# Units first in their step, a later combining pass, and a rearranged prologue in a fused spectral-mixing and ELU kernel

## The chip, the cores and the metric

The kernel runs on one core of a Trainium2 chip. The core has five engines with queues of their own: TensorE (PE in the profile, with its weight loads as PEld), VectorE (DVE), ScalarE (ACT), GpSimd (POOL) and SyncE (SP), the last of which only issues DMA transfers here. POOL and ACT issue some transfers too. Each engine works its own instructions in the order in which the program lists them; engines wait for each other by semaphores. The metric is device time in microseconds for one execution of the whole program.

## The reference

Two stages follow each other. The first takes x (8 batches, 3008 positions, 256 channels), transforms it along the positions, multiplies by a complex 256x256 matrix, adds a bias, shrinks each part towards zero by 0.01, and transforms back. The second is a two-layer network with an ELU between the layers, on all 24064 rows.

```python
X = np.fft.rfft(x, axis=1)                      # x: 8, 3008, 256
Yr = Xr @ w_r - Xi @ w_i + b_r
Yi = Xr @ w_i + Xi @ w_r + b_i
Yr = np.sign(Yr) * np.maximum(np.abs(Yr) - 0.01, 0.0)
Yi = np.sign(Yi) * np.maximum(np.abs(Yi) - 0.01, 0.0)
y = np.fft.irfft(Yr + 1j * Yi, n=3008, axis=1)
...
h = y.reshape(24064, 256) @ w_in                # w_in: 256, 2048
g = np.where(h > 0.0, h, np.exp(np.minimum(h, 0.0)) - 1.0)
out = g @ w_out                                 # w_out: 2048, 256
```

## The kernel before, in words

3008 is 47 x 64, and the transform is done in two short matrix products per direction. One batch goes through five kinds of units, each of which fills one PSUM slot of two banks with matmuls and has it emptied ("evicted") by another engine:

- A (`unit_A`, L112; 8 a batch): x times the table M1, two matmuls of 512 columns. ACT evicts to a tile A, and SP writes A to a DRAM buffer DA (L134, L136), two units a write.
- X (`unit_X`, L148; 6 a batch): a tile Z is read back from DA in another order (`load_Z`, L138), in three groups of eight frequencies; Z times the table M2, eight matmuls of 128 columns. ACT evicts to XT.
- M (`unit_M`, L183; 12 a batch, M(q, i)): XT times the complex weights wcat, four matmuls of 512 columns; DVE adds the bias (yb, L179), POOL clips and subtracts (L187, L188). Two M units share one PSUM slot.
- B (`unit_B`, L210; 6 a batch): the shrunk values times the table M3, eight matmuls on halves of the array's rows (64 rows each). ACT evicts to Bz, SP writes Bz to a DRAM buffer DB.
- Y (`unit_Y`, L252; 8 a batch): Bs is read back from DB (`load_Bs`, L243), Bs times M4, eight matmuls of 94 columns. ACT evicts to yT, which the second stage reads.

The second stage runs in 48 steps a batch (`PER`): six blocks of 512 rows (the last has 448), eight pairs of 128 hidden channels each. In step i, `front(i)` (L529) makes the hidden values hps of one pair with four matmuls of 512 columns, and ACT takes their exponential into Et (L547). `elu(i)` (L550) makes gT from both in two passes over 1024 elements on DVE: a first pass on Et alone (L558; in steps without a unit, L555 splits it between DVE and POOL) and a combining pass that reads hps too (L559 or L556) and so frees its PSUM slot. `back(i-2)` (L567) multiplies the gT of two steps ago by w_out into an accumulator ps_o (eight matmuls of 256 columns, L584). Every eighth step ACT copies ps_o to osb, and SP writes that out in four or five transfers.

hps has two PSUM slots, ps_o two of one bank each, and all the units together have one slot (`psF`). So a unit can start only when the one before it has been evicted, and hps of step i only when the combining pass of step i-2 is done.

The units of the next batch, and the A units of the one after that, are laid into the steps of this batch by `plan(b)` (L616), which gives each step three lists: f0 is issued ahead of `front`, f1 between `front` and `elu`, f2 behind `back` (the loop at L675 to L694). X and Y stand in f0; A, M and B in f1; the loads of Bs, the last loads of Z and one Y unit in f2. The order on each engine is the order in which this loop issues. In batch 0, two Y units, the eight A units of batch 1, four Y units and then the list `mid` follow each other, from step 1 on; the loads of x for batch 2 are listed in steps 13, 16, 19 and 22 (`xs`). POOL, which issues them, has nothing else to do before and reaches them early.

Ahead of the loop lies a prologue. POOL issues the loads of x for batch 0 and makes index tables; DVE makes phases from them (three groups, L383 to L395, with `wrap` for the range reduction), ACT the sines (L362); in between, the eight A units of batch 0 run. Then Z is loaded, and X, M and B of batch 0 run with eviction shared out between ACT and DVE (`fX`, `first_M`, `fB`, L466 to L500). Matmuls on dummy data (`idle_pe`) fill PE's waits. After B, Bs is loaded, the first two Y units run (L508), a gate on POOL (L511) waits for part of Bs, and behind it the four x tiles of batch 1 are loaded (L512).

Of the kernel before, what the change touches and what calls it, by code (L numbers as in the profile page):

```python
# [8 lines left out]
ALU = mybir.AluOpType  # L9
# [16 lines left out]
def kernel(  # L26
# [38 lines left out]
    xp = ctx.enter_context(tc.tile_pool(name="xp", bufs=4))  # L65
    wk2 = ctx.enter_context(tc.tile_pool(name="wk2", bufs=2))
# [27 lines left out]
    def load_x(b, ci):  # L94
        xv = x[b].rearrange("(r m c) d -> c r m d", c=4, m=8)
# [16 lines left out]
    def unit_A(b, u, alone=False, on_dve=False):  # L112
# [9 lines left out]
        dav = DA_of[b].rearrange("(m c) r d -> c r m d", c=4)  # L122
# [15 lines left out]
    def load_Z(b, g, engs=None):  # L138
        engs = engs or (nc.sync, nc.sync)
        Z = wk3.tile([P, 8, D], BF16, name="Z", tag="Z")  # L140
        for c in range(2):
            for h in range(2):
                r = h * 2 * K1 + c * K1 + 8 * g
                q = c * N2 + h * NH
                engs[c].dma_start(Z[q : q + NH], DA_of[b][:, r : r + 8, :])
        Z_of[b, g] = Z

    def unit_X(b, u, alone=False, on_dve=False):  # L148
# [3 lines left out]
        XT, Z = XT_of[b, g], Z_of[b, g]  # L152
        ps = unit_ps("xps", alone)
        psv = ps[:].rearrange("p a (k j) -> p (a k) j", j=P)
        for kk in range(8):
            nc.tensor.matmul(  # L156
                psv[:, kk, :], lhsT=Z[:, kk, dt * P : dt * P + P], rhs=M2[:, :, 8 * g + kk, :],
                start=True, stop=True,
            )
        evac(  # L160
            XT[:, dt].rearrange("p c (k j) -> p c k j", j=N2),
            psv.rearrange("p k (c j) -> p c k j", c=2), on_dve,
        )
# [79 lines left out]
    def load_Bs(b, w, engs=None):  # L243
        engs = engs or (nc.sync, nc.sync)
        Bs = wk4.tile([4 * K1, 8, D], BF16, name="Bs", tag="Bs")
        dv = DB_of[b].rearrange("k (c m) d -> (k c) m d", c=2)
        for h in range(2):
            n0 = h * NH + 8 * w
            engs[h].dma_start(Bs[h * 2 * K1 : h * 2 * K1 + 2 * K1], dv[:, n0 : n0 + 8, :])
        Bs_of[b, w] = Bs  # L250
# [28 lines left out]
    with tc.tile_pool(name="stagep", bufs=1) as stagep:  # L279
# [3 lines left out]
        w_r_f = stagep.tile([P, 2, D], F32, name="w_r_f")  # L283
        nc.sync.dma_start(w_r_f[:], w_r.rearrange("(c p) e -> p c e", p=P))
        w_i_f = stagep.tile([P, 2, D], F32, name="w_i_f")
        nc.sync.dma_start(w_i_f[:], w_i.rearrange("(c p) e -> p c e", p=P))
# [16 lines left out]

        pcol = iota([P, 1], "pcol", [[0, 1]], cm=1)
        k1row = iota([2 * N1, 2, K1], "k1row", [[0, 2], [1, K1]])
        ph1 = iota([2 * N1, 2, K1], "ph1", [[QUARTER, 2], [0, K1]], base=QUARTER)
        for ci in range(2):
            load_x(0, ci)
        kv = iota([P, K1, N2], "kv", [[1, K1], [N1, N2]])
        for ci in range(2, 4):  # L310
            load_x(0, ci)
# [413 lines left out]
```

## Time and profile before

| | us |
|---|---|
| median of three runs | 972.80 (972.73 to 973.07) |
| the profiled execution | 972.56 |
| its span in the profile | 970.8 |
| first hps matmul of the loop | 65.28 |
| first hps of batches 1, 2, 3, 4, 5, 6, 7 | 193.88, 307.40, 420.84, 534.30, 647.80, 761.27, 871.37 |
| busy time PE, DVE, ACT, POOL | 932.9, 799.6, 634.0, 316.7 |

A step is the time from one first hps matmul to the next. By these starts a steady batch takes 113.5 us, batch 0 128.6, batch 6 (which has no A units to run) 110.1, and batch 7 (which has only Y units) 99.4 with the end of the program. In a step, a busy time is not a limit in itself: the chain of waits tells which engine the next one waited for. Groups of PE matmuls overlap at their ends in the timeline, so slots on PE are read from the chain, or from start to start.

### The profile page before, as it was taken

Reading aid. Unit: us, or ns where it says so; the run is one execution under the profiler, and the core shown is the slowest. Engines: PE = TensorE matmul, PEld = TensorE weight load, DVE = VectorE, ACT = ScalarE, POOL = GpSimd, SP = SyncE. Lnnn points to the kernel's source line nnn. Section 1 sums busy time; section 2 is a strip of 40 time slices with the busy share of each in tenths; the row PEclk is TensorE's granted clock in tenths of the full one; section 3 lists DMA queues with packets and bytes.
Section 4 is the critical chain, followed back from the end, with each engine's and each line's share of the span. In section 5 each row is a group of like instructions: output and inputs, shape, how many; then the busy total and the mean of one; then the engine's idle time right before and its main releaser. Section 6 shows DMA issues by size and latency. Waiting matters only on the chain.

```text
span 970.8 us, 16851 instructions
## 1 busy us (share of the span) xinstructions
PE 932.9 (96%) x6507; PEld 659.5 (68%) x6507; DVE 799.6 (82%) x935; ACT 634.0 (65%) x724; POOL 316.7 (33%) x359
## 2 busy tenths in 40 slices
PE   6887999999999999999999999999999999999997
PEld 2445766676667766776667766777667776677775
DVE  8555888788878888888888888788888888888896
ACT  4445755876687666775676756876667756667564
POOL 4341155026402443117312264024431053321332
PEclk8898999999999999999999999999999999999999
DMA  9979461847157452755437482574517301331011
GB/s 192 266 158 206 120 109 48 200 113 130 54 147 162 77 88 59 191 106 86 83 97 200 70 132 55 139 167 76 93 52 194 78 22 51 89 80 42 23 44 41
DMA packets 115331, 105.43 MB, mean 109 GB/s; under 512 B 8242, under 2 KB 108084, under 8 KB 115252
## 3 DMA queue, kind: packets, MB, share of 16 engines
q1 hardware_dynamic: 87028, 76.05, 29.9%
q0 software_dynamic: 27680, 26.74, 20.5%
q10 hardware_dynamic: 544, 1.57, 0.6%
q8 instruction: 51, 0.84, 0.4%
q14 instruction: 28, 0.23, 0.1%
HBM read 54.53 MB, written 49.81 MB: 107 GB/s over the span
## 4 chain that ended last, share of the span: by engine, by line
PE 63%; DVE 19%; ACT 9%; issue 4%; DMA 3%; POOL 2%; DVEq 0%; ACTq 0%; POOLq 0%
PE ps_o L584 25%; PE hps L542 24%; DVE gT L556 7%; PE mps L172 7%; ACT Et L547 5%; DVE gT L559 3%; DVE Et L555 3%; PE xps L156 2%; DVE Et L558 2%; PE aps L125 2%; PE bps L220 2%; PE yps L260 1%; DVE yb L179 1%; DMA DA<-A 1%; ACT A L110 1%
## 5 line engine op out<-in xcount | busy, mean ns | idle before, releaser
L547 ACT ACTIVATE Et<-hps 128x1024 f32<-128x1024 f32 (+1 forms) x384 | 388.1, 1011 | 220.7 <-PE hps L542 217.1
L584 PE MATMUL ps_o<-w_out_r,gT 128*128 128x256 f32 (+1 forms) x3072 | 479.9, 299 | 1.1 <-DVE gT L556 1.0
L584 PEld LDWEIGHTS ps_o<-w_out_r,gT 128*128 128x128 f32 (+1 forms) x3072 | 408.9, 187 | 62.3 <-DVE gT L556 13.0
L542 PE MATMUL hps<-yT,w_in_s 128*128 128x512 bf16 (+1 forms) x1536 | 391.0, 377 | 3.6 <-DVE gT L556 1.0
L559 DVE SCALAR_TENSOR_TENSOR gT<-hps,Et 128x1024 fp32r<-128x1024 f32 (+1 forms) x287 | 348.9, 1216 | 24.4 <-DVE Et L558 0.5
L558 DVE TENSOR_SCALAR Et<-Et 128x1024 f32<-128x1024 f32 (+1 forms) x287 | 204.4, 712 | 86.3 <-ACT Et L547 82.4
L542 PEld LDWEIGHTS <-w_in_s 128*128 128x128 bf16 x1536 | 125.3, 98 | 108.6 <-issue 6.3
L187 POOL TENSOR_SCALAR clip<-yb 128x512 f32<-128x512 f32 x84 | 82.1, 977 | 324.1 <-DVE yb L179 322.2
L555 POOL TENSOR_SCALAR Et<-Et 128x512 f32<-128x512 f32 (+1 forms) x97 | 62.1, 640 | 262.0 <-ACT Et L547 262.0
L556 DVE SCALAR_TENSOR_TENSOR gT<-Et,hps 128x1024 fp32r<-128x1024 f32 (+1 forms) x97 | 112.6, 1160 | 21.2 <-POOL Et L555 11.0
L188 POOL TENSOR_TENSOR Y<-yb,clip 128x512 bf16<-128x512 f32 x84 | 108.5, 1292 | 7.0
L110 ACT CAST XT<-xps 128x1024 bf16<-128x1024 f32 x46 | 46.6, 1012 | 52.8 <-PE xps L156 52.8
L179 DVE TENSOR_TENSOR yb<-mps,bias_bc 128x512 f32<-128x512 f32 x96 | 65.6, 687 | 9.4 <-PE mps L172 5.1
L110 ACT CAST A<-aps 96x1024 bf16<-96x1024 f32 x63 | 62.9, 1003 | 13.0 <-PE aps L125 7.8
L172 PEld LDWEIGHTS <-XT 128*128 128x128 bf16 x384 | 37.3, 98 | 44.8 <-issue 1.4
L110 ACT CAST yT<-yps 128x752 bf16<-128x752 f32 x63 | 49.6, 788 | 25.5 <-PE yps L260 25.5
L125 PE MATMUL aps<-xt,M 94*96 94x512 f32 x128 | 50.2, 478 | 13.9 <-ACT A L110 10.1
L172 PE MATMUL mps<-wcat_r,XT 128*128 128x512 bf16 x192 | 57.6, 382 | 0.0
L172 PE MATMUL mps<-wcat_s,XT 128*128 128x512 bf16 x192 | 57.2, 380 | 0.0
L555 DVE TENSOR_SCALAR Et<-Et 128x512 f32<-128x512 f32 (+1 forms) x97 | 52.1, 537 | 2.7 <-ACT Et L547 2.7
L596 ACT COPY osb<-ps_o 128x512 f32<-128x512 f32 x88 | 47.5, 590 | 8.0 <-PE ps_o L584 8.0
L98 POOL DMA_DIRECT2D xt<-in_x_dram x64 | 44.3, 694 | 12.0 <-PE aps L125 11.6
(83 smaller groups left out, 338.9 us busy)
## 6 DMA issues: line engine op xcount, KB each, us to landing
xt<-in_x_dram POOLq DMA_DIRECT2D x32, 640.0 KB, 6.0
out_dram<-osb SPq DMA_DIRECT2D x160, 128.0 KB
Z<-DA SPq DMA_DIRECT2D x90, 128.0 KB
Bs<-DB SPq DMA_DIRECT2D x60, 192.0 KB
DA<-A SPq DMA_DIRECT2D x28, 384.0 KB
DB<-Bz SPq DMA_DIRECT2D x21, 512.0 KB
xt<-in_x_dram POOLq DMA_DIRECT2D x32, 112.0 KB, 5.7
w_in_f<-in_moe_w_in_dram SPq DMA_DIRECT2D x4, 512.0 KB
```

Source lines behind the costliest of these rows:

```text
L110: nc.scalar.copy(dst, src)
L172: nc.tensor.matmul(ps, lhsT=XT[:, dt, c, o : o + P], rhs=wm[:, dt, :], start=(m == 0 and dt == 0), stop=(m == 1 and dt == 1),)
L179: nc.vector.tensor_tensor(yb[:], ps, bias_bc[:], ALU.add)
L187: nc.gpsimd.tensor_scalar(clip[:], yb[:], LAM, -LAM, ALU.min, ALU.max)
L188: nc.gpsimd.tensor_tensor(Y_of[b, q][:, i, :], yb[:], clip[:], ALU.subtract)
L542: nc.tensor.matmul(hps[:, s, 0:nb], lhsT=w_in_s[:, dt, ft * P : ft * P + P], rhs=yT[:, dt, bs : bs + nb], start=(dt == 0), stop=(dt == 1),)
L547: nc.scalar.activation(Et[:, :, 0:nb], hps[:, :, 0:nb], AF.Exp)
L555: eng.tensor_scalar(E_[:, s], E_[:, s], 1.0, 0.0, ALU.min, ALU.max)
L556: nc.vector.scalar_tensor_tensor(gT[:, :, 0:nb], E_, -1.0, h_, ALU.add, ALU.max)
L558: nc.vector.tensor_scalar(E_, E_, 1.0, -1.0, ALU.min, ALU.add)
L559: nc.vector.scalar_tensor_tensor(gT[:, :, 0:nb], h_, 0.0, E_, ALU.max, ALU.add)
L584: nc.tensor.matmul(po[q][0 : t1 - t0, i_ % 2, :], lhsT=gT[:, s, t0:t1], rhs=w_out_r[:, ft, :], start=(ft == 0 and i_ % 2 == 0), stop=(ft = ...
```

## The change

1. Order in the loop. All units now stand in f0, ahead of `front`. The combining pass of step i-1 (`finish_elu`) is issued in step i, behind the units and `front`, so behind a bias pass of an M unit of step i; behind it comes the first pass of step i. f2 is gone: load_Bs follows A(2) and load_Z follows A(7), in f1.
2. Batch 0. The Y units 6 and 7 move from before X(0) of batch 1 to places between later units. A gate on POOL, which waits for the last group of Z of batch 1, stands ahead of the x loads of batch 2. Both of Y(1, 0) and Y(1, 1) are in f0.
3. Layout. The 32 rows that belong to one r are split into four consecutive runs of eight (`r c m`) instead of every fourth row (`r m c`). A tile of x then reads 8 KB in one piece per partition, and the rows of DA that one tile fills lie together (`c m`).
4. Prologue tables. The second phase table is made as an absolute value and a product with half the range (two operations of one pass) instead of a shift and a second `wrap`; all three groups come first on DVE, ahead of the small tables. The sines are issued in single halves between the A units. Of the x loads, only the first is ahead of the table kv on POOL.
5. Z is one tile of 24 frequencies for the whole batch (pool zp). In batch 0, its first half (from the first two tiles of A) is loaded on POOL's queue after A(3), the second in three groups on SP and ACT. The loads of w_r and w_i come after A(3), and their casts to wcat go from POOL to DVE.
6. In the prologue, each X eviction is split in halves between ACT and DVE, and X and M units alternate from M(0, 0) on. The first 16 frequencies of Bs for w = 0 and 1 are loaded before B(5), the rest after it.

```diff
     def load_x(b, ci):
-        xv = x[b].rearrange("(r m c) d -> c r m d", c=4, m=8)
+        xv = x[b].rearrange("(r c m) d -> c r m d", c=4, m=8)
...
-        dav = DA_of[b].rearrange("(m c) r d -> c r m d", c=4)
+        dav = DA_of[b].rearrange("(c m) r d -> c r m d", c=4)
...
-    def load_Z(b, g, engs=None):
-        engs = engs or (nc.sync, nc.sync)
-        Z = wk3.tile([P, 8, D], BF16, name="Z", tag="Z")
+    def load_Z(b, k0, k1, n0, n1, engs):
+
+        if b not in Z_of:
+            Z_of[b] = zp.tile([P, K1, D], BF16, name="Z", tag="Z")
         for c in range(2):
             for h in range(2):
-                r = h * 2 * K1 + c * K1 + 8 * g
+                r = h * 2 * K1 + c * K1
                 q = c * N2 + h * NH
-                engs[c].dma_start(Z[q : q + NH], DA_of[b][:, r : r + 8, :])
-        Z_of[b, g] = Z
+                engs[c].dma_start(
+                    Z_of[b][q + n0 : q + n1, k0:k1, :], DA_of[b][n0:n1, r + k0 : r + k1, :]
+                )
...
+        if alone:
+            nc.scalar.copy(xv[:, :, 0:4], pv[:, :, 0:4])
+            nc.vector.tensor_copy(xv[:, :, 4:8], pv[:, :, 4:8])
+        else:
+            nc.scalar.copy(xv, pv)
...
-    def load_Bs(b, w, engs=None):
+    def load_Bs(b, w, k0=0, k1=K1, engs=None):
...
-        for ci in range(2):
-            load_x(0, ci)
+        load_x(0, 0)
         kv = iota([P, K1, N2], "kv", [[1, K1], [N1, N2]])
-        for ci in range(2, 4):
+        for ci in range(1, 4):
             load_x(0, ci)
...
+        def phases(g):
+
+            gs = slice(8 * g, 8 * g + 8)
+            nc.vector.tensor_scalar(
+                v2[:, gs, :], kv[:, gs, :], n2col[:], ph2col[:], ALU.mult, ALU.add
+            )
+            nc.vector.tensor_scalar(
+                st[:, gs, :], kv[:, gs, :], S // 2 + 0.5, -0.5, ALU.is_gt, ALU.add
+            )
+            v = flat(v2[:, gs, :])
+            wrap(v, flat(r2[:]))
+            nc.vector.scalar_tensor_tensor(flat(r2[:]), v, -1.0, v, ALU.mult, ALU.max)
+            nc.vector.scalar_tensor_tensor(
+                flat(u2[:, gs, :]), flat(r2[:]), -float(QUARTER), flat(st[:, gs, :]),
+                ALU.add, ALU.mult,
+            )
...
+        for g in range(3):
+            phases(g)
...
-        for g in range(3):
-            gs = slice(8 * g, 8 * g + 8)
...
-            for c in range(2):
-                wrap(flat(v2[:, c, gs, :]), flat(r2[:, c]))
-            unit_A(0, 2 * g, alone=True)
-            unit_A(0, 2 * g + 1, alone=True)
-            if g < 2:
-                idle_pe(5)
-            else:
-                idle_pe(3)
-                unit_A(0, 6, alone=True)
-                unit_A(0, 7, alone=True, on_dve=True)
-                idle_pe(6)
-            sines(g)
+        sines(0, 0)
+        unit_A(0, 0, alone=True)
+        unit_A(0, 1, alone=True)
+        sines(0, 1)
+        idle_pe(4)
+        unit_A(0, 2, alone=True)
+        unit_A(0, 3, alone=True)
+        load_Z(0, 0, K1, 0, NH // 2, (nc.gpsimd, nc.gpsimd))
+        nc.sync.dma_start(w_r_f[:], w_r.rearrange("(c p) e -> p c e", p=P))
+        nc.sync.dma_start(w_i_f[:], w_i.rearrange("(c p) e -> p c e", p=P))
+        sines(1, 0)
+        sines(1, 1)
+        idle_pe(4)
+        unit_A(0, 4, alone=True)
+        unit_A(0, 5, alone=True)
+        sines(2, 0)
+        sines(2, 1)
+        idle_pe(2)
+        unit_A(0, 6, alone=True)
+        unit_A(0, 7, alone=True, on_dve=True)
...
-            load_Z(0, g, (nc.sync, nc.scalar))
+            load_Z(0, 8 * g, 8 * g + 8, NH // 2, NH, (nc.sync, nc.scalar))
...
-        idle_pe(5)
-        nc.gpsimd.tensor_copy(wcat_r[:, :, 0:D], w_r_f[:])
...
+        idle_pe(9)
+        nc.vector.tensor_copy(wcat_r[:, :, 0:D], w_r_f[:])
...
     fX(0)
-    fX(1, True)
+    fX(1)
+    first_M(0, 0, True)
     fX(2)
-    fX(3, True)
-    first_M(0, 0, True)
+    first_M(0, 1, False)
+    fX(3)
+    first_M(1, 0, True)
     fX(4)
-    first_M(0, 1, False)
+    first_M(1, 1, False)
     fX(5)
...
     fB(4)
+    for w in range(2):
+        load_Bs(0, w, 0, 16)
     fB(5, True)
     for w in range(4):
-        load_Bs(0, w, (nc.sync, nc.scalar))
+        load_Bs(0, w, 16 if w < 2 else 0, K1, (nc.sync, nc.scalar))
...
+    late_elu = []
+
+    def finish_elu():
+        for i, hps, Et, nb, on_pool in late_elu:
+            E_, h_ = Et[:, :, 0:nb], hps[:, :, 0:nb]
+            gT = late3.tile([P, 2, TB], F32R, name="gT", tag="gT")
...
+            g_of[i] = gT
+        late_elu.clear()
...
         else:
             nc.vector.tensor_scalar(E_, E_, 1.0, -1.0, ALU.min, ALU.add)
-            nc.vector.scalar_tensor_tensor(gT[:, :, 0:nb], h_, 0.0, E_, ALU.max, ALU.add)
-        g_of[i] = gT
+        late_elu.append((i, hps, Et, nb, on_pool))
...
-                [("y", 2), ("y", 3)] + [("a", u) for u in range(8)]
-                + [("y", u) for u in range(4, 8)] + mid
-            )
+                [("y", 2), ("y", 3)] + [("a", u) for u in range(8)] + [("y", 4), ("y", 5)] + mid
+            )
+            seq.insert(25, ("y", 6))
+            seq.insert(29, ("y", 7))
...
+            f1[xs[0]].append((lambda: gate(Z_of[1][:, 16, 0:1]), ()))
...
             h = front(i, calm and bare % 3 == 2)
+        finish_elu()
+        if i < n:
             for f, a in f1[r]:
                 f(*a)
             elu(i, *h, on_pool=free and i > 0)
         if i >= LAG:
             back(i - LAG)
-        if i < n:
-            for f, a in f2[r]:
-                f(*a)
```

## The prediction

> **What bounds the kernel now.** I read the page first, then the chain of waits in a steady batch, then the timeline where steps are longer than their slots, then the first 112 us.
>
> ```profile
> span 970.8 us, 16851 instructions
> PE 932.9 (96%) x6507; PEld 659.5 (68%) x6507; DVE 799.6 (82%) x935; ACT 634.0 (65%) x724; POOL 316.7 (33%) x359
> ```
>
> TensorE (PE) is the bound. A "step" is one front plus one back, from one first `hps` matmul to the next. The chain at 446 to 484 us (start, duration, what) gives clean PE slots: hps 0.88 (0.86 behind X), ps_o 0.95, M 0.86, X 0.46, B 0.54.
>
> ```profile
> 450.70 0.54 PE bps L220 x8
> 451.25 1.14 PE ps_o L584 x8
> 452.39 1.02 PE hps L542 x4
> 453.41 0.86 PE mps L172 x4
> 454.27 0.93 PE ps_o L584 x8
> ```
>
> Behind B, ps_o takes 1.14 instead of 0.95 and the next hps 1.02 instead of 0.88. The timeline shows the other losses of a batch, X waiting for a bias pass (`yb`) and Y for B's eviction:
>
> ```profile
> 447.41 0.61 PE L156 MATMUL xps<-M,Z 128*128 128x128 bf16 x8 [0.23 <-DVE yb L179]
> 483.88 0.49 PE L260 MATMUL yps<-M,Bs 96*128 96x94 bf16 x8 [0.34 <-ACT Bz L233]
> ```
>
> Prologue and batch 0: the loop begins at 65.28 and loses time near 90 us, on DA's landing. X(0) waits for Z at 33.28.
>
> ```profile
> 24.98 1.21 DVE L108 CAST A<-aps 96x1024 bf16<-96x1024 f32 x1
> 33.28 1.86 PE L156 MATMUL xps<-M,Z 128*128 128x128 bf16 x16 [3.37 <-DMA Z<-DA]
> 89.93 1.01 ACT L110 CAST A<-aps 96x1024 bf16<-96x1024 f32 x1 [5.09 <-DMA DA<-A]
> ```
>
> The windows' last column (GB/s): x loads (6:16 and 70:82) move slower than w_out's (42:48) or Z's (30:36).
>
> ```profile
> 6.00:16.00 10.00, 6.19 (x26) 2.54 (x24) 7.29 (x20) 2.59 (x4) 6.26 (x10) 1.00 2.01 208
> 42.00:48.00 6.00, 6.00 (x40) 2.55 (x39) 5.14 (x8) 4.30 (x6) 4.93 (x6) 1.00 1.78 355
> 30.00:36.00 6.00, 1.86 (x16) 1.73 (x17) 0.82 (x1) 1.01 (x1) 0.00 (x0) 0.70 0.98 262
> 70.00:82.00 12.00, 11.20 (x66) 7.65 (x65) 9.24 (x10) 8.08 (x9) 4.73 (x7) 1.00 1.98 214
> ```
>
> **The change part by part.**
>
> *x's rate.* A row's share of a tile becomes one run of 8 KB instead of eight of 1 KB. Bounds: 208 GB/s (as now) and 355 (w_out's loads, 1 KB pieces). I take 262, from Z's loads in 4 KB pieces, the longest shown: 2.9 us per 770 KB tile instead of 3.7.
>
> *Prologue up to X(0).* Before, DVE builds the tables from 10.73 to 25.06, 4.56 us a group (15.85 to 20.41), with the last A eviction behind them, to 26.19. After: per group v 0.54, st 0.42, one wrap 0.42+0.43+0.69, absolute value 0.69, u 0.69 = 3.88, packed like the old ones (4.56 for a sum of 4.73) 3.74, so 11.2 for three. They start behind M1 (6.51): 17.7. The small operations moved behind them (8.98 to 10.73, 1.75) give 19.5, the eviction 1.21: 20.7. ACT agrees: from 9.0 six sines of 0.63 and seven evictions of 1.0, 20 to 21. From there 2.5 to the Z issue (26.22 to 28.70), then Z in half the bytes, 3.9 instead of 4.6 (28.70 to 33.28): X(0) at 27.1, gain 6.2. Low end: DMA carries more ahead of X(0): x 3.1 MB, DA 1.6, half of Z 0.8, w_r and w_i 0.5, at 208 GB/s 29 us from about 2, X(0) at 31, gain 2. High end 8 (Z's second half in 2.5). wcat's four casts go to DVE (w_in's casts: 2.49 for four of twice the size, so about 1.3); cover: DVE is idle from 29.45 to 35.18 while Z loads. The moved w_r and w_i loads stand on SP behind A(3)'s writes and have till then. The half of Z on POOL's queue holds up only the gate and the w_out load.
>
> *X(0) to the first step* (32.0 us). X evictions are halved: six DVE casts of 0.69 instead of two of 1.23, 1.7 more on a DVE that sets the pace there (2.37 a pair of M), but M(0,0) starts two evictions earlier (1.23 and the serial wait, about 2). Net 0.3 gain, bounds -2 and +2. Bs in parts would save about 1 of the 4.2 from issue (59.68) to Y (63.84), but the 28 idle matmuls ahead of Y on PE run until 63.80: taken as 0. The early Bs loads wait on SP for DB(3) (about 55.5: issue 53.12 and 2.3 as from 57.34 to 59.68) and take four issues of 0.42; queued behind them is DB(5)'s write (57.34), late by 0 to 0.3.
>
> *Batch 0, step 3 (72.56) to X(0) of batch 1 (109.47), 36.9 us.* x loads begin at the gate (67.3) and are drained 2+4x2.9 = 13.8 later, at step 3 + 8.5. DA(0) is queued behind them, lands at about 10.5 and is wanted at 9.8: stall 0.7. Without x of batch 2 in front the 5.1 us stall goes, and the slow clock behind it (PE groups at 91 to 95 took 1.17, 1.71, 1.73 for 0.46, 0.95, 0.88). But what is late next is Z: X(0) comes two steps sooner, y6 and y7 being moved behind. The last A starts at 8 steps of 2.28 less one, 16.0; its eviction now stands behind the two output copies of step 9 (18.6) and its DMA behind their four issues on SP (2.6 us): 19.7. DA to Z's first group took 7.1 before (issue 100.76, Z issue 104.20, the trace's packets of that group end at 107.49): 26.8. X(0) is due at 23.0: stall 3.8, and 2.0 for a slow clock behind it (0 to 2.3, by the groups above). New: 23.0+0.7+3.8+2.0, and 4.3 for the two Y steps now later = 33.8. Gain 3.1. Bounds: -2 (x at 208) and +9 (nothing late).
>
> The Trainium skill (DMA: Bandwidth & Descriptors, Queues, rings and completion order) says that a DMA engine serves its queues in turn, packet by packet; then x on POOL's queue could not hold back DA on SP's, and holding x back would be worth nothing. The row says otherwise: DA issued at 78.90, behind x of 77.68, landed after 10.93, against 3.44 at 100.76. By the page the 5.1 stays and this term is -2.
>
> The new gate in step 13 holds POOL until Z's last group lands; behind it stand the x loads of batch 2 (wanted in step 37) and the clip of M(0,0) two steps on, whose B comes six steps later: 0.
>
> *Step 46 of batch 0:* A(7) and Y(0) share a PSUM slot, 4.53 before. Y(0) then waits for an eviction that no longer stands behind Exp: 0.3 gain.
>
> *Steady batches.* Order on PE becomes unit, hps, ps_o; on ACT eviction, Exp; on DVE yb(r), combine(r-1), first pass(r). Step lengths of batch 3 (113.46) against slots:
> - X behind M: 3.15, 3.50, 3.20, 3.20 against 0.88+0.86+0.95+0.46 = 3.15. yb now runs before the combining pass: 0.45.
> - Y behind B: 3.38 against 0.88+0.54+1.14+0.35 = 2.91; B's eviction no longer stands behind Exp: 0.47.
> - Steps 20 and 5 (2.09, 1.93 against 1.81) wait for a combining pass; a unit now stands ahead of the hps concerned: 0.40.
> - B: 0.19 on ps_o six times and 0.14 on hps twice, 1.42 in all. In the prologue M follows B after 0.55 and takes its usual 0.87, so hps behind B should pay nothing; ps_o to B is not shown. Bounds 0 and 1.42, taken 1.0.
> - Steps 33 to 35 (A with two output copies, 1.08 on ACT; 0.45 lost now): the copies delay an eviction, then Exp, then a combining pass: 0.2 worse.
> - M steps (2.68) and single Y steps (2.16) stay. load_Bs one step sooner waits on SP for DB; the A write behind it is 1.5 us later, with two steps to spare.
>
> Sum 2.1 a batch: batches 1 to 5 10.6, batch 6 1.9 (no A), batch 0 1.4, batch 7 0: 13.9. Bounds 5 (no B gain, osb twice as bad) and 19.
>
> The Trainium skill (TensorEngine Tiling (Array Packing), Key Properties) says that a change of tiling mode drains the array. B runs as two 64-row tiles and changes the mode twice wherever it stands; by that page its gain is 0 and the sum 6.5 smaller.
>
> *Sum:* 6.2+0.3+3.1+0.3+13.9 = 23.8, off the profiled execution's 972.56 (span 970.8 plus 1.8): 948.8. The median is 0.24 above that run: 949.
>
> **The rivals.**
> 1. x stays at 208 GB/s. For: the partition count and row pitch of its loads are the same. Against: w_out, in as short pieces, made 355. Prologue gain 2.8, batch 0 -1.5: 957.
> 2. The steady gain stays at its low end, 5: waits return in another place, and B pays on its other side: 958.
> 3. Slower: eviction before Exp makes a loop. In an X step the chain is eviction at +0.66, Exp +1.57, first pass +2.63, combine +3.43 to +4.66 (X at 431.62); hps two steps on is due at 2x2.27+0.45 = 4.99. A is 0.06 later: slack 0.2. Should yb, POOL's hold on DVE or a late Exp stretch it by more than 0.2, each of some 28 unit steps a batch loses half the excess. At 0.45 the 196 steps lose 24 us and all is eaten; at 0.5, 977. For: ACT runs 2.06 in 2.27 us there, and X(0) already loses 0.23 behind three Y steps. Against: the same order holds for X and Y today at 2.16 to 2.28.
> 4. Z of batch 1 is in time and B gains all: 3.1 becomes 8.9, 13.9 becomes 17: 940.
>
> **How the numbers follow.** As summed 0.50 (943 to 955), rival 1 0.16, rival 2 0.14, rival 3 0.10, rival 4 0.10. The range 938 to 962 leaves out rival 3 and the edges. A measurement of this kernel tells 0.2% (2 us) from no change. Slower has rival 3 alone (0.10), same 0.02, faster 0.88.
>
> **What would show it.** First hps at 58 to 60; X(0) at 27. B steps at 2.4, the step with B and Y at 2.7, a batch at 111.3 instead of 113.46. In step 13 X(0) waiting 3 to 4 us for Z, and no wait for DA above 1 us. x loads above 250 GB/s. A wait "hps <- DVE gT" of tenths in many steps is rival 3; a prologue whose X(0) starts after 30 makes 949 wrong by itself.

## The result, and the profile after

| | before | after | ratio (95% interval) |
|---|---|---|---|
| median, us | 972.93 (972.73 to 973.35, 4 runs) | 1020.26 (1017.21 to 1022.64, 4 runs) | 1.048 (1.045 to 1.052) |
| the profiled execution, us | 972.56 | 1021.8 | |
| its span, us | 970.8 | 1020.0 | |

The changed kernel is 47 us slower. 949 was forecast, with 0.10 for slower. By the first hps of each batch, the change of 49.2 us between the two spans lies here (us, minus is a gain; the columns add up to the spans):

| stretch | forecast | after minus before | the version with five places put right, minus before |
|---|---|---|---|
| start to X(0) | -6.2 | -0.1 | -6.0 |
| X(0) to the first hps | -0.3 | +2.4 | +2.0 |
| batch 0 | -4.8 | +11.3 | -4.9 |
| batches 1 to 5 | -10.6 | +32.6 | -12.1 |
| batch 6 | -1.9 | +3.2 | -1.3 |
| batch 7 and the end | 0 | -0.2 | -0.4 |

The last column is a run from the experiments (the subtract held, Z and Bs whole) that keeps the new step order, the new tables and the new layout of x. Each figure rests on one profiled execution of a version, and in the first two stretches versions with the same code there differ by 1 to 2.5 us. So a gain of the size of the forecast is there to be had from these parts, and something else costs some 70 us. The page of the changed kernel (span, busy time by engine, and the chain that ended last by engine):

```profile
span 1020.0 us, 16866 instructions
PE 943.6 (93%) x6502; PEld 664.6 (65%) x6502; DVE 850.5 (83%) x937; ACT 639.7 (63%) x726; POOL 278.0 (27%) x360
PE 40%; DVE 36%; DMA 8%; ACT 8%; issue 4%; POOL 1%; SPq 1%; DVEq 0%; ACTq 0%; POOLq 0%
```

DVE is busy 51 us longer with two instructions more, and POOL is busy 39 us less. The chain by engine and the groups of the page of before, which the prediction did not show, are these (after the bar: busy time in us, mean ns of one):

```profile
PE 63%; DVE 19%; ACT 9%; issue 4%; DMA 3%; POOL 2%; DVEq 0%; ACTq 0%; POOLq 0%
L558 DVE TENSOR_SCALAR Et<-Et 128x1024 f32<-128x1024 f32 (+1 forms) x287 | 204.4, 712 | 86.3 <-ACT Et L547 82.4
L187 POOL TENSOR_SCALAR clip<-yb 128x512 f32<-128x512 f32 x84 | 82.1, 977 | 324.1 <-DVE yb L179 322.2
L555 POOL TENSOR_SCALAR Et<-Et 128x512 f32<-128x512 f32 (+1 forms) x97 | 62.1, 640 | 262.0 <-ACT Et L547 262.0
```

and the same groups of the changed kernel, with hps:

```profile
L566 PE MATMUL hps<-yT,w_in_s 128*128 128x512 bf16 (+1 forms) x1536 | 396.5, 381 | 27.4 <-DVE gT L585 24.8
L598 DVE TENSOR_SCALAR Et<-Et 128x1024 f32<-128x1024 f32 (+1 forms) x287 | 265.6, 926 | 86.7 <-ACT Et L571 83.3
L194 POOL TENSOR_SCALAR clip<-yb 128x512 f32<-128x512 f32 x84 | 51.6, 614 | 352.9 <-DVE yb L186 228.0
```

The first pass of the ELU is the same instruction on the same data, and its mean went from 712 to 926 ns: 61 us in all. POOL's clip went the other way, from 977 to 614 ns. And hps now waits 24.8 us for the combining pass (gT). The timeline of two M units in the fourth steady batch shows how (start, duration, engine, line, what; in brackets the idle time before it and what ended that):

```profile
582.11 1.21 DVE L585 SCALAR_TENSOR_TENSOR gT<-hps,Et 128x1024 fp32r<-128x1024 f32 x1
582.29 0.61 POOL L194 TENSOR_SCALAR clip<-yb 128x512 f32<-128x512 f32 x1 [15.21 <-DVE yb L186]
582.98 1.27 POOL L195 TENSOR_TENSOR Y<-yb,clip 128x512 bf16<-128x512 f32 x1
583.42 1.38 DVE L598 TENSOR_SCALAR Et<-Et 128x1024 f32<-128x1024 f32 x1
...
586.19 1.27 POOL L195 TENSOR_TENSOR Y<-yb,clip 128x512 bf16<-128x512 f32 x1
586.45 1.55 DVE L598 TENSOR_SCALAR Et<-Et 128x1024 f32<-128x1024 f32 x1
586.59 1.04 PE L566 MATMUL hps<-yT,w_in_s 128*128 128x512 bf16 x4 [0.16 <-DVE gT L585]
```

The combining pass now stands between the bias pass and the first pass. While it runs, POOL does its clip undisturbed; when the first pass is due, POOL is in its subtract, and the first pass takes 1.4 to 1.55 us instead of 0.69. Two steps on, hps waits for a combining pass that this made late. X steps behind an M pair take 2.59 to 2.88 us (an X step that stands free 2.28), Y steps 2.80 (2.16); most M steps stay at 2.69.

The second place is on SP, late in each batch: before (first fence) and after (second), the write of A to DA against the loads of Bs.

```profile
506.44 0.33 SPq L136 DMA_DIRECT2D DA<-A  x1
510.01 3.81 SPq L249 DMA_DIRECT2D Bs<-DB  x8
```

```profile
652.68 3.58 SPq L258 DMA_DIRECT2D Bs<-DB  x8
656.35 0.38 SPq L137 DMA_DIRECT2D DA<-A  x1
...
662.84 1.01 ACT L111 CAST A<-aps 96x1024 bf16<-96x1024 f32 x1 [3.23 <-DMA DA<-A]
```

In the changed kernel the eight Bs loads go ahead of the A write. A later eviction into the same A buffer waits 3.23 us for that write; step 36 takes 4.5 to 5.7 us instead of 2.3, and PE runs slowly in the step or two behind it (2.4 to 3.4 us instead of 1.8 to 2.3). The write could have gone out at 654.05, when the eviction before it ended; it was issued 2.3 us later and then took 6.4 us more to land. PE's granted clock was 0.50 at 666 to 668 us. In batch 0 the same place costs more: the eviction of A(6) waits 8.51 us, and step 45 takes 12.25.

The third place is the start:

```profile
20.02 1.22 DVE L109 CAST A<-aps 96x1024 bf16<-96x1024 f32 x1 [2.19 <-PE aps L126]
20.36 1.97 POOL L147 DMA_DIRECT2D Z<-DA  x4 [11.33 <-DMA DA<-A]
...
29.34 3.53 SPq L147 DMA_DIRECT2D Z<-DA  x6
33.14 1.86 PE L160 MATMUL xps<-M,Z 128*128 128x128 bf16 x16 [4.49 <-DMA Z<-DA]
...
65.72 0.83 PE L270 MATMUL yps<-M,Bs 96*128 96x94 bf16 x16 [2.35 <-DMA Bs<-DB]
67.58 1.41 PE L566 MATMUL hps<-yT,w_in_s 128*128 128x512 bf16 x4 [1.04 <-DVE yT L109]
```

The tables and the last A eviction are done at 21.24 (20.02 and 1.22), 5 us sooner than before (26.19), close to the forecast (20.7). But the second half of Z is issued only at 29.34, 8 us behind the last write of DA (21.27; before, 26.22 to 28.70), and X(0) starts at 33.14, where it started before.

And the fourth, X(0) of batch 1 in batch 0, two steps sooner in the order than before:

```profile
104.25 1.01 PE L160 MATMUL xps<-M,Z 128*128 128x128 bf16 x8 [4.50 <-DMA Z<-DA]
```

### The profile page after: what moved, and what is told of

It reads as the page before. It is cut to its first block, busy times and chain, and to the rows that moved or that the text cites. A ratio compares the mean times of both kernels' runs of the same rounds, so it can differ in the third digit from the quotient of the medians.

```text
span 1020.0 us, 16866 instructions
## 1 busy us (share of the span) xinstructions
PE 943.6 (93%) x6502; PEld 664.6 (65%) x6502; DVE 850.5 (83%) x937; ACT 639.7 (63%) x726; POOL 278.0 (27%) x360
## 3 DMA queue, kind: packets, MB, share of 16 engines
q1 hardware_dynamic: 87060, 75.92, 28.2%
## 4 chain that ended last, share of the span: by engine, by line
PE 40%; DVE 36%; DMA 8%; ACT 8%; issue 4%; POOL 1%; SPq 1%; DVEq 0%; ACTq 0%; POOLq 0%
PE hps L566 18%; PE ps_o L623 14%; DVE gT L585 12%; DVE Et L598 10%; DVE gT L581 7%; DMA DA<-A 5%; ACT Et L571 5%; PE mps L179 4%; DVE yb L186 4%; DVE Et L596 3%; PE aps L126 2%; PE yps L270 1%; DMA xt<-in_x_dram 1%; PE bps L227 1%; ACT A L111 1%
## 5 line engine op out<-in xcount | busy, mean ns | idle before, releaser
L623 PE MATMUL ps_o<-w_out_r,gT 128*128 128x256 f32 (+1 forms) x3072 | 496.7, 304 | 1.0 <-DVE gT L581 1.0
L623 PEld LDWEIGHTS ps_o<-w_out_r,gT 128*128 128x128 f32 (+1 forms) x3072 | 415.6, 189 | 61.6 <-DVE gT L581 12.9
L566 PE MATMUL hps<-yT,w_in_s 128*128 128x512 bf16 (+1 forms) x1536 | 396.5, 381 | 27.4 <-DVE gT L585 24.8
L598 DVE TENSOR_SCALAR Et<-Et 128x1024 f32<-128x1024 f32 (+1 forms) x287 | 265.6, 926 | 86.7 <-ACT Et L571 83.3
L566 PEld LDWEIGHTS <-w_in_s 128*128 128x128 bf16 x1536 | 134.2, 99 | 178.7 <-issue 51.8
L194 POOL TENSOR_SCALAR clip<-yb 128x512 f32<-128x512 f32 x84 | 51.6, 614 | 352.9 <-DVE yb L186 228.0
L111 ACT CAST A<-aps 96x1024 bf16<-96x1024 f32 x63 | 63.5, 1013 | 42.9 <-DMA DA<-A 28.2
L126 PE MATMUL aps<-xt,M 94*96 94x512 f32 x128 | 42.7, 422 | 24.2 <-ACT A L111 20.1
L240 ACT CAST Bz<-bps 128x1024 bf16<-128x1024 f32 x47 | 47.5, 1011 | 19.1 <-PE bps L227 19.1
L170 ACT CAST XT<-xps 128x1024 bf16<-128x1024 f32 x42 | 42.5, 1012 | 21.7 <-PE xps L160 21.7
L179 PEld LDWEIGHTS <-XT 128*128 128x128 bf16 x384 | 30.3, 98 | 28.7 <-issue 1.1
## 6 DMA issues: line engine op xcount, KB each, us to landing
out_dram<-osb SPq DMA_DIRECT2D x160, 128.0 KB
Z<-DA SPq DMA_DIRECT2D x84, 128.0 KB
```

Of the source, the lines that this page charges most:

```text
L111: nc.scalar.copy(dst, src)
L126: nc.tensor.matmul(ps[0 : 4 * K1, j, :], lhsT=M1[:], rhs=xt[:, 4 * uu + 2 * j : 4 * uu + 2 * j + 2, :], start=True, stop=True,)
L179: nc.tensor.matmul(ps, lhsT=XT[:, dt, c, o : o + P], rhs=wm[:, dt, :], start=(m == 0 and dt == 0), stop=(m == 1 and dt == 1),)
L566: nc.tensor.matmul(hps[:, s, 0:nb], lhsT=w_in_s[:, dt, ft * P : ft * P + P], rhs=yT[:, dt, bs : bs + nb], start=(dt == 0), stop=(dt == 1),)
L598: nc.vector.tensor_scalar(E_, E_, 1.0, -1.0, ALU.min, ALU.add)
L623: nc.tensor.matmul(po[q][0 : t1 - t0, i_ % 2, :], lhsT=gT[:, s, t0:t1], rhs=w_out_r[:, ft, :], start=(ft == 0 and i_ % 2 == 0), stop=(ft = ...
```

## The experiments

Two theories stood at the outset. By the first (P), POOL's subtract holds the first pass, since the combining pass moved between it and the bias pass. By the second (S), the order on SP makes the A write late. The rival for the steady batches was rival 3 without either: the chain of eviction, Exp, first pass and combining pass is too long by itself once units go first, so that units first is what costs (in the expectations this is theory U; theory N is that the A write is late for another reason). The ratios are to the kernel before as timed beside the runs: 973.9 us for the first four, 972.7 for the others.

**The combining pass back behind its own first pass, units still first.**

```diff
         late_elu.append((i, hps, Et, nb, on_pool))
+        finish_elu()
```

> The changed kernel with one thing undone: the combining pass of a step follows its own first pass at once again (units still first). Theory P (the late combining pass puts DVE's first pass beside POOL's subtract, and the two hinder each other): the first pass falls from a mean of 926 ns to about 710, batch 6 (no A units) from 113.3 to 108-110 us, the time from 1020 to about 990. Theory U (units first is what hurts, by a chain eviction, Exp, first pass, combining pass, next hps): the first pass may get shorter but the steps stay at 2.7 to 2.85, time above 1012.

Measured: 999.16, ratio 1.026 (1.023 to 1.029), 21 us less than the changed kernel, where some 30 less had been expected. The first pass is at 717 ns again; X steps take 2.27, Y 2.16, B 2.43 to 2.46. Step 36 still takes 4 us and more. But the second M of a pair takes 3.0 us:

```profile
569.75 1.23 DVE L585 SCALAR_TENSOR_TENSOR gT<-hps,Et 128x1024 fp32r<-128x1024 f32 x1
...
570.89 0.68 DVE L186 TENSOR_TENSOR yb<-mps,bias_bc 128x512 f32<-128x512 f32 x1
...
571.58 0.69 DVE L598 TENSOR_SCALAR Et<-Et 128x1024 f32<-128x1024 f32 x1
571.63 0.59 PE L179 MATMUL mps<-wcat_r,XT 128*128 128x512 bf16 x2 [0.19 <-DVE yb L186]
571.67 1.07 POOL L194 TENSOR_SCALAR clip<-yb 128x512 f32<-128x512 f32 x1 [16.47 <-DVE yb L186]
```

The bias pass now queues behind the combining pass, and the next M waits for it. So the late combining pass had a use; what hurt is what it made coincide. The clip, which starts 0.09 behind the first pass here, takes 1.07 instead of 0.61, and the first pass nothing more than its 0.69: the one that starts first is not held. In 42 of the 84 M units it goes this way; in 41 the clip starts first, and there the first pass takes 868 ns on the mean.

**Bs loads behind A(3) again.**

```diff
-            if u == ("A", 2):
+            if u == ("A", 3):
```

> The changed kernel with one thing undone: the four loads of Bs follow A(3), not A(2). Theory S (the 1.5 MB of Bs stand ahead of the write of the second A tile, on SP and in the DMA engines, and the fourth A tile waits for that write): step 36 falls from 4.5-5.7 to 2.3 us, the slow clock behind it goes, batches 1 to 5 lose 4 to 6 us each, step 45 of batch 0 falls from 12.3 to about 4; time about 987. Theory N (A is late for another reason, the A units being faster in a row now): step 36 stays above 4, time above 1012.

Measured: 992.54, ratio 1.019 (1.016 to 1.022): 28 us less. The first pass is still at 926 ns. Batches 1 to 5 take 115.6 to 116.1 instead of 118.8 to 121.6, batch 0 132.5 instead of 139.9. (In the profiled execution the first hps is 1.7 us earlier too, at a place that this edit does not touch.)

```profile
632.59 0.33 SPq L137 DMA_DIRECT2D DA<-A  x1
633.03 4.38 SPq L258 DMA_DIRECT2D Bs<-DB  x8
...
640.87 1.01 ACT L111 CAST A<-aps 96x1024 bf16<-96x1024 f32 x1 [0.38 <-PE aps L126]
```

In batches 1 to 5 no A eviction waits for DA, and step 36 takes 2.27 to 2.29; batch 0 keeps two such waits, of 1.8 and 1.6 us. S is shown, and it is independent of P.

**No subtract on POOL.**

```diff
-        nc.gpsimd.tensor_scalar(clip[:], yb[:], LAM, -LAM, ALU.min, ALU.max)
-        nc.gpsimd.tensor_tensor(Y_of[b, q][:, i, :], yb[:], clip[:], ALU.subtract)
+        nc.gpsimd.tensor_scalar(Y_of[b, q][:, i, :], yb[:], LAM, -LAM, ALU.min, ALU.max)
```

> The changed kernel with POOL's second operation of an M unit in the loop left out: the clipped value itself is written as the result, in one operation with one input, so the shrinking is not computed. Order and all else as in the change. Theory P, and it is the two-input subtract that hinders: first pass at 680 to 750 ns, batch 6 at 108-110, time about 990. Theory U: first pass may fall, time above 1012. If POOL's clip is what hinders, the first pass stays at about 0.9 or more.

This version leaves the subtraction out, so the shrinking is not computed. Measured: 983.73, ratio 1.010 (1.007 to 1.013), 36.5 us less, with the Bs loads still too early. Nothing of DVE's work or order was touched, and its first pass is back at its undisturbed time:

```profile
L597 DVE TENSOR_SCALAR Et<-Et 128x1024 f32<-128x1024 f32 (+1 forms) x287 | 197.6, 689 | 99.2 <-ACT Et L570 91.9
```

All M steps take 2.69, X steps behind an M pair 2.27, Y 2.16, B 2.45. Batch 6, which has no A units and so nothing of S, takes 108.55; forecast was 110.1 - 1.9 = 108.2. That the chain is too long by itself (the rival) falls with this run.

**The late combining pass alone, in the kernel before.** Here units still follow `front`.

```diff
...
             for f, a in f1[r]:
                 f(*a)
-            elu(i, *h, on_pool=free and i > 0)
+        finish_elu()
+        if i < n:
+            elu(i, *h, on_pool=free and i > 0)
```

> The kernel before with one part of the change alone: the combining pass of a step is issued behind the bias pass of the next. Theory P: the first pass rises from 712 to 850-950 ns, each M step or its neighbour gets longer by some tenths, time 990 to 1005. Theory U: the order of the passes alone does no harm, time 968 to 977.

Measured: 1080.35, ratio 1.110 (1.106 to 1.113), much more than expected: M steps take 3.80 to 3.88 us. The first pass takes 942 ns on the mean, as theory P has it.

```profile
480.30 1.02 PE L542 MATMUL hps<-yT,w_in_s 128*128 128x512 bf16 x4
...
482.22 0.69 DVE L179 TENSOR_TENSOR yb<-mps,bias_bc 128x512 f32<-128x512 f32 x1 [0.98 <-PE mps L172]
482.83 1.22 DVE L561 SCALAR_TENSOR_TENSOR gT<-hps,Et 128x1024 fp32r<-128x1024 f32 x1
...
484.10 1.04 PE L542 MATMUL hps<-yT,w_in_s 128*128 128x512 bf16 x4 [0.98 <-DVE gT L561]
```

Most of the loss is a loop that the expectation had left out: hps, then M behind it on PE, then the bias pass, then the combining pass queued behind it, which frees the slot that the next hps needs. One turn, from hps to hps, is 3.80. With units ahead of `front` the M does not wait for that hps and the loop is open. So the two halves of part 1 of the change go together, and this run prices neither alone.

**The subtract held until the first pass is over, and Bs behind A(3).** Everything is computed.

```diff
-        nc.gpsimd.tensor_tensor(Y_of[b, q][:, i, :], yb[:], clip[:], ALU.subtract)
+        shrink.append((Y_of[b, q][:, i, :], yb, clip))
...
+    def finish_shrink(Et):
+        for Y_, yb, clip in shrink:
+            gate(Et[:, 0, 0:1])
+            nc.gpsimd.tensor_tensor(Y_, yb[:], clip[:], ALU.subtract)
+        shrink.clear()
...
             elu(i, *h, on_pool=free and i > 0)
+            finish_shrink(h[1])
...
-            if u == ("A", 2):
+            if u == ("A", 3):
```

> Same arithmetic as the changed kernel; two edits: the Bs loads go back behind A(3), and POOL's subtract is held until the first pass of the same step is over (POOL reads one element of the first pass's result ahead of it), so that it runs beside the bias pass and the combining pass. If the subtract hurts only the first pass (theory P): first pass 0.69 to 0.72 us on the mean, M steps 2.7, batches 1 to 5 at 111 to 112, and the time is the 983.7 of the run without a subtract less the 28 of the run with Bs behind A(3): 953 to 959. If DVE loses time to any pass of POOL wherever it lies (rival): the combining or the bias pass grows by what the first pass lost, M steps stay at 2.8 to 3.0 and the time is near the 992.5 of the run with Bs alone, 985 to 995.

Measured: 960.47, ratio 0.988 (0.986 to 0.990). The time is 1.5 us above the range that was expected; the first pass is at 700 ns, batches 1 to 5 at 111.0 to 111.1, batch 6 at 108.7. The timeline of an M pair:

```profile
543.59 0.61 POOL L194 TENSOR_SCALAR clip<-yb 128x512 f32<-128x512 f32 x1 [15.24 <-DVE yb L186]
544.72 0.69 DVE L606 TENSOR_SCALAR Et<-Et 128x1024 f32<-128x1024 f32 x1
...
545.48 0.69 DVE L186 TENSOR_TENSOR yb<-mps,bias_bc 128x512 f32<-128x512 f32 x1
545.62 1.28 POOL L202 TENSOR_TENSOR Y<-yb,clip 128x512 bf16<-128x512 f32 x1
546.09 1.21 DVE L593 SCALAR_TENSOR_TENSOR gT<-hps,Et 128x1024 fp32r<-128x1024 f32 x1
```

The subtract runs beside the bias pass and the combining pass, which both read PSUM, and neither side is longer than alone (0.69, 1.21, 1.28). So it is not POOL's work as such that costs DVE time, but which of DVE's passes it meets. What sets the first pass apart from the other two (its operation, or where its inputs lie) these runs do not separate. The rival of this expectation (any pass of DVE loses) falls.

**Does the number of POOL's inputs matter?** In the changed kernel the subtract is replaced by a copy of clip, so the shrinking is not computed.

```diff
-        nc.gpsimd.tensor_tensor(Y_of[b, q][:, i, :], yb[:], clip[:], ALU.subtract)
+        nc.gpsimd.tensor_scalar(Y_of[b, q][:, i, :], clip[:], 1.0, 0.0, ALU.mult, ALU.add)
```

> The changed kernel with POOL's subtract replaced by a pass of one input that only copies the clipped values (the shrinking is not computed), at the same place and beside the same first pass. If two inputs on POOL are what holds the first pass: first pass 0.69 to 0.75 us, time 983 to 990. If any pass of POOL that starts ahead of the first pass holds it: first pass stays at 0.85 or more in the mean, and the time above 1000.

Measured: 985.66 (one run), the first pass at 712 ns. By the expectation's wording that is "two inputs", but the trace does not bear the conclusion: the copy takes 0.62 instead of 1.27 and is nearly over when the first pass begins. These are the first passes over 1024 elements that overlap a pass of POOL that began sooner; the last column is over the 690 to 693 ns of first passes without overlap in the same run:

| kernel | POOL's pass | count | overlap, ns | first pass, ns | longer by, ns |
|---|---|---|---|---|---|
| changed kernel | subtract, two inputs | 84 | 962 | 1510 | 820 |
| combining pass back at once | clip, one input | 41 | 323 | 868 | 175 |
| one-input run | copy, one input | 84 | 229 | 775 | 82 |

In all three the first pass loses the overlap less 0.14 to 0.15 us, with one input as with two. So the copy was cheap because it was short, and the number of inputs is not what decides; an overlap as long as the subtract's with a one-input pass wasn't tried. The Trainium skill (SBUF — State Buffer, Who interferes with whom) says the same in a stronger form: a DVE instruction in a two-port mode, such as `tensor_scalar` can have, and a GpSimd instruction share a pair of ports, "whoever issues first gets the shared pair for the whole instruction", and the other waits. These runs agree within the 0.15 us: the 84 clips of before, which begin inside a first pass, take 977 ns instead of 614 and leave it at 683. That the first pass runs in a two-port mode is not shown here.

**Z and Bs whole, Y(4) to Y(7) ahead of X(0), on top of the held subtract.**

```diff
-        load_Z(0, 0, K1, 0, NH // 2, (nc.gpsimd, nc.gpsimd))
...
-            load_Z(0, 8 * g, 8 * g + 8, NH // 2, NH, (nc.sync, nc.scalar))
+            load_Z(0, 8 * g, 8 * g + 8, 0, NH, (nc.sync, nc.scalar))
...
-    for w in range(2):
-        load_Bs(0, w, 0, 16)
...
-        load_Bs(0, w, 16 if w < 2 else 0, K1, (nc.sync, nc.scalar))
+        load_Bs(0, w, 0, K1, (nc.sync, nc.scalar))
...
-            seq.insert(25, ("y", 6))
-            seq.insert(29, ("y", 7))
```

(and `("y", 4)` to `("y", 7)` follow the eight A units, as before the change)

> The run with the subtract held and Bs behind A(3), and with three more edits of the change undone, each in a place of its own: Z of batch 0 is loaded whole on SP and ACT after A(7)'s write (no half on POOL's queue), Bs of batch 0 is loaded whole after B(5), and Y(4) to Y(7) of batch 0 stand ahead of X(0) again. If Z's half on POOL's queue is what ate the prologue's gain: X(0) at 27 to 29 instead of 33.1. If it was the shorter chain of tables itself that brings nothing: X(0) at 33. If the early Bs loads held DB(5)'s write: Y(0) 1 to 2 us sooner after the last B than in the changed kernel (DB pair 46.3 to 49.6 us there). If X(0) of batch 1 only moved into a wait for Z: the two steps that wait now 11.4 us together lose 4 to 5, and batch 0 comes to 124 to 128 us. All three: 943 to 949. None: the time of the run with the subtract held.

Measured: 948.81 (947.10 to 949.85, 4 runs), ratio 0.975 (0.973 to 0.977).

```profile
23.08 3.83 SPq L147 DMA_DIRECT2D Z<-DA  x6
...
27.31 1.86 PE L160 MATMUL xps<-M,Z 128*128 128x128 bf16 x16 [3.22 <-DMA Z<-DA]
...
59.42 0.84 PE L278 MATMUL yps<-M,Bs 96*128 96x94 bf16 x16 [1.51 <-DMA Bs<-DB]
...
61.30 1.04 PE L571 MATMUL hps<-yT,w_in_s 128*128 128x512 bf16 x4 [1.04 <-DVE yT L109]
```

Z is issued 3.0 us behind the last write of DA (20.08) instead of 8.1, and X(0) starts at 27.31; the forecast for it was 27.1. So the shorter tables do bring the 6 us, and the half of Z on POOL's queue had eaten them: in the six profiled versions that have it X(0) starts at 31.7 to 34.2, in the three that load Z whole and x in long runs at 27.3 to 28.1. X(0) of batch 1 waits for nothing (the steps of X(0) and X(1) take 2.43 and 2.28 instead of 7.01 and 4.29 in the run with the subtract held), and batch 0 takes 123.7. Whole Bs loads bring little: X(0) to the first hps is 34.0 instead of 34.4. That 948.81 falls on the 949 of the forecast confirms nothing of the changed kernel: four of its edits are undone here and the subtract is placed anew.

**x of batch 2 not held back.** In that version the gate on POOL is taken out.

```diff
-            f1[xs[0]].append((lambda: gate(Z_of[1][:, 16, 0:1]), ()))
```

> The run with everything held and whole, without the wait of x of batch 2 for Z (POOL's gate in step 13 of batch 0 is taken out). If transfers issued earlier on POOL's queue stand ahead of DA's on SP's queue, as the row of 10.93 us of before was read: the wait of 5 us for DA returns in batch 0 (A's eviction, or X(0) for Z), batch 0 at 127 to 131 us instead of 123.6, the whole 3 to 7 us slower, 951 to 956. If the queues are served in turn: batch 0 within 1 us, 948 to 950.

Measured: 955.15, ratio 0.982 (0.980 to 0.984). Batch 0 takes 128.0 instead of 123.7, and the wait for DA, 2.46 us with the gate (first fence), is back to more than the 5.09 of before (second):

```profile
82.11 1.01 ACT L111 CAST A<-aps 96x1024 bf16<-96x1024 f32 x1 [2.46 <-DMA DA<-A]
```

```profile
86.96 1.01 ACT L111 CAST A<-aps 96x1024 bf16<-96x1024 f32 x1 [7.97 <-DMA DA<-A]
```

So transfers issued earlier on POOL's queue do hold up a later write on SP's, and the row of before was the right thing to go by. The Trainium skill (DMA: Bandwidth & Descriptors, Queues, rings and completion order) has each DMA engine serve its queues in turn, a packet at a time. The prediction had drawn from it that the write would not be held at all; that conclusion falls. The rule itself, by which the write shares the engines, is neither shown nor refuted by this run.

**x in runs of 1 KB, as before.** The two patterns of part 3 of the change are put back in that version.

```diff
-        xv = x[b].rearrange("(r c m) d -> c r m d", c=4, m=8)
+        xv = x[b].rearrange("(r m c) d -> c r m d", c=4, m=8)
...
-        dav = DA_of[b].rearrange("(c m) r d -> c r m d", c=4)
+        dav = DA_of[b].rearrange("(m c) r d -> c r m d", c=4)
```

> The run with everything held and whole, with x in runs of 1 KB as before (and DA's rows in before's order). If the run length sets the rate of x: 207 GB/s instead of 230 to 245 while x of batch 0 loads, X(0) 1 to 2 us later than 27.3, batch 0 1 to 2 us longer, in all 950 to 953. If it does not: 948 to 950.

Measured: 950.55 (950.24 to 950.86), ratio 0.977 (0.975 to 0.979). The window of 6 to 16 us (the last column is GB/s) of the changed kernel and of this run:

```profile
6.00:16.00 10.00, 7.77 (x32) 3.42 (x30) 9.62 (x20) 6.78 (x9) 2.95 (x5) 1.00 1.15 229
```

```profile
6.00:16.00 10.00, 7.08 (x27) 3.08 (x26) 9.66 (x20) 5.94 (x8) 2.98 (x6) 0.85 2.02 199
```

In the version with long runs, 234 GB/s stand there. So the length of the run does move x's rate; X(0) comes 2.1 us later (29.40 instead of 27.31) and the first hps 1.1 (62.44 instead of 61.30). But batch 0 takes 123.0, 0.7 less than with long runs, against the expectation, and the two profiled spans differ by 0.4 us (948.5 and 948.1) where the medians differ by 1.7. What the layout is worth to the whole, between nothing and 2 us, is left open.

**The first X and M units in before's order.** Each X is evicted by one engine again, and M(0, 0) stands behind X(3).

```diff
-        if alone:
-            nc.scalar.copy(xv[:, :, 0:4], pv[:, :, 0:4])
-            nc.vector.tensor_copy(xv[:, :, 4:8], pv[:, :, 4:8])
-        else:
-            nc.scalar.copy(xv, pv)
+        evac(xv, pv, on_dve)
...
-    fX(1)
-    first_M(0, 0, True)
+    fX(1, True)
     fX(2)
-    first_M(0, 1, False)
-    fX(3)
-    first_M(1, 0, True)
+    fX(3, True)
+    first_M(0, 0, True)
     fX(4)
+    first_M(0, 1, False)
...
```

> The run with everything held and whole, with the first X and M units in before's order and each X evicted by one engine (X(1) and X(3) by DVE) as before. There X(0) to the first hps took 32.0 us, in the changed kernel 34.4 and in the run with everything whole 34.0. If the halved evictions and the earlier M(0,0) are what lengthens the stage: 32 to 32.5, and 946.5 to 947.5. If it is the loads of w_in and w_out or the clock: 34, and 948 to 949.

Measured: 946.29 (945.97 to 948.89, 4 runs), ratio 0.974 (0.972 to 0.976), the fastest version here; its runs overlap with those of the version with the new order.

```profile
28.10 1.06 PE L160 MATMUL xps<-M,Z 128*128 128x128 bf16 x16
...
58.02 1.24 PE L567 MATMUL hps<-yT,w_in_s 128*128 128x512 bf16 x4 [0.60 <-ACT yT L111]
```

X(0) to the first hps takes 29.9 us, less than the 32.0 expected at best. Part of the 4.1 that it gains on the same version with the new order goes with the clock: in the first 2 us from X(0) on the granted clock was 1.00 here and 0.50 there, and X(0)'s matmuls took 1.06 and 1.86. The run without x held back has the new order and a granted clock of 1.00 at X(0), and takes 32.8 from X(0), at 27.95, to the first hps, 1.2 less. So the halved evictions and the earlier M cost 2.9 us on like terms, by one profiled execution of each.

## Why the prediction was wrong, point by point

The 47 us are close to 28 (Bs, SP) + 32 (subtract, from 992.5 to 960.5) + 12 (Z, Bs and Y in batch 0, from 960.5 to 948.8) - 24 (what is left as gain, from 972.7 to 948.8). The prices are those of this order of undoing; with the Bs loads still early, leaving the subtract out was worth 36.5.

- **The steady batches.** The terms of the 2.1 a batch for X, Y and B came about as priced (2.27, 2.16, 2.45) in the version without the two disturbances, where a batch takes 111.1 and 111.3 was forecast. So B steps did gain (2.54 to 2.71 before), against the reading that set its gain at 0; and steps 33 to 36, with the output copies, are 0.3 better (9.3 instead of 9.6) where 0.2 worse was forecast. What failed is the first line under the steady batches, "on DVE yb(r), combine(r-1), first pass(r)", with no look at what POOL does meanwhile. The clip and the subtract start with yb and take 1.9 us; before, the 0.69 of the first pass met the clip, which had the worse of it (977 ns); now the combining pass of 1.2 lies between, and the first pass meets the subtract. The page of before had the hint: POOL's clip and its share of the first pass are one operation on the same size and type, and took 977 and 640 ns. M steps stayed at 2.69, as forecast; it is the next X, Y or B step that pays.
- **Rival 3** named the place, "Should yb, POOL's hold on DVE or a late Exp stretch it by more than 0.2", and its sign, with a chance of 0.10. Its sign came, hps waiting for gT, 24.8 us in all. The stretch was 0.82 on 84 first passes. The chain's slack of 0.2 was known, and the overlap could have been worked out from three durations; it was left as a doubt instead of a sum. Its wording of the loop (196 steps) is not what happened; without POOL's subtract the chain has room enough.
- **Bs one step sooner**, "waits on SP for DB; the A write behind it is 1.5 us later, with two steps to spare": the second large miss, 28 us. The issue was priced (1.5, measured 2.3) and the transfer was not. The eight loads (1.5 MB by the page's size of an issue, 192 KB) are issued ahead of the A write, which lands 6.4 us behind its own issue, and the next eviction into that A buffer waits for it. In batch 0, five output transfers of osb stand ahead of it too.
- **Prologue to X(0).** The tables' end (20.7 forecast, 21.2 measured) and X(0) (27.1, and 27.3 once Z is whole) were right. What failed is "The half of Z on POOL's queue holds up only the gate and the w_out load". It was issued at 20.36, ahead of the last write of DA (21.27), which landed at 29.2. The same text used a row in batch 0 in which loads on POOL's queue hold back DA's writes, and did not apply it 60 us earlier. That the low bound of 2 was missed (0.1) has the same cause.
- **X(0) to the first hps.** 0.3 gain was taken with bounds of 2 either way; measured 2.4 loss. "M(0,0) starts two evictions earlier (1.23 and the serial wait, about 2)" is the term that failed. M(0,0) is indeed earlier (its bias pass 4.0 us behind X(0) instead of 6.5), but the last bias pass is at 21.2 instead of 19.8: the lead is gone by the end of the M units, and the 1.7 more on DVE is there. Bs in parts at 0 was about right (0.4 worse): DB(5)'s write was issued 2.35 us behind DB(4)'s instead of 1.84, late by 0.5 and not by 0 to 0.3.
- **Batch 0, step 3 to X(0) of batch 1.** Right in its sizes: X(0) at 28.2 us (forecast 23.0 + 0.7 + 3.8 = 27.5), 1.9 lost behind it in the step of X(1), at a granted clock of 0.50 (2.0), so a gain of 2.5 with the two Y steps behind (3.1 forecast). Behind x the wait for DA was 1.7 (0.7). The wait for Z had been seen as 3.8 and was kept as a price; with the Y units left in front of X(0) it is not there at all, and the stretch gains 8.1 (28.8 against 36.9).
- **Step 46 of batch 0.** The 0.3 did not come: this is the place where the Bs loads cost most (12.25 in step 45), and in the version with the five places put right A(7)'s step takes 4.70 where it took 4.53.
- **x at 262 GB/s**: 229 measured. The nearest row was not Z's but x's own before (208): a longer run in the same transfer moved it by a tenth (208 to 229) to a sixth (199 to 234).

## What to carry to other kernels

When a pass is moved on one engine, write down what the engines beside it do in that microsecond, above all GpSimd beside VectorE: one operation on one size with two mean times in a profile (here 977 and 640 ns on POOL) is a reason to look at what runs beside it; here two engines held each other up, and the one that started second paid. When a load is moved ahead of a write on a queue, price its bytes, not its issue, and go on to who waits for the write to land. And if one row of a trace shows that one queue's transfers hold up another's, hold every other place of the change against that row.

## What was not expected of the hardware

A VectorE first pass lost 0.82 us to 0.96 us of overlap with a GpSimd subtract that had begun before it; one that begins first loses nothing (means of 683 and 694 ns) and the GpSimd pass waits instead (614 to 977 and 1105 ns). The bias pass and the combining pass, which read PSUM, lost nothing beside the same subtract (0.69 and 1.21 us). Half of Z, 0.8 MB, moved from DA to 16 partitions at a time on POOL's queue took from 20.36 to 30.45 us, some 80 GB/s counted from its first issue to its last landing; whole, in 32 partitions a transfer on the queues of SP and ACT, Z moved at 262 to 344 GB/s in the windows of 1 us from 25 to 28 us.
